# Routing tables of a fused attention and mixture-of-experts kernel: joined on VectorE instead of GpSimd, with earlier first weights for expert 0

## The chip, the cores and the metric

One core of one Trainium2 chip runs the whole kernel. The metric is device time of that core in microseconds, the median of several executions.

## What is computed

Eight batches of eight heads of attention over 576 positions with 64 elements each. Four heads see the last 32 positions, four see every fourth of the last 128. The result is read as 4608 rows of 512 elements, and each row goes through one of eight experts, the one with the largest gate logit:

```python
logits = x @ w_gate
expert_idx = np.argmax(logits, axis=1)
...
    xe = x[mask]
    h = np.maximum(xe @ w1[e], 0.0)
    ye = h @ w2[e]
    out[mask] = gate_w[mask, None] * ye
```

`w1[e]` is 512x1024, `w2[e]` is 1024x512, `gate_w` the softmax probability of the chosen expert.

## The kernel before

**Attention.** Two batches form a pair, four pairs (`NPR`) of nine tiles (`NT`) of 128 positions: 36 steps (`total`). `step(n)` (L1102) is a hand-written software pipeline: scores of tile n, softmax and transposes of n-1, products with v of n-2, transposes of the finished rows x of n-3, gate logits of n-4. TensorE, VectorE and ScalarE keep the written order in the first 35 steps (`MEND`, L1154); GpSimd and SP, and all engines from step 35 on, get their order from the framework's scheduler, which goes by readiness and by place in the program. Within a step, small jobs are pulled from lists: `side` (routing, pulled by `pull_off` and `pull_pe`), `slow` (scatters, two a step), `spare` (weight splits, one a step).

**Routing.** `route(m)` (L455) runs once per pair, from step 12, 21, 30 and 39. It turns the logits, finds the expert, counts the places within each expert with three matrix products, and for pairs 0 to 2 scatters (row number, gate) into three tables in device memory, `tabs`, in turn (L524, with the place computed by `place`, L518). Three tables are there so that a scatter waits only for the third one before it; empty entries are zero, so that the tables are joined by adding. The last pair takes another way: for each of its nine tiles `mark` (L536) makes two one-hot operands, `s1` (L539, from `ca`) and `b1` (L547), `enter` (L552) multiplies them on TensorE into the PSUM tile `tb`, VectorE scales `tb` (L634, L638) and adds it to the joined rows, which gives `row_i` (L639; the trace shows that line as L428). From `row_i` all experts but the first blocks of expert 0 gather their rows (L735).

**The tables.** `read_table` (L648) reads the three tables on SP's queue into `t_in[0..2]`, 128x320x2 int32 (row and gate). `add_tables` (L653) joins them with three GpSimd instructions: t0+t1 (L656), rows (L657), gates into `base` (L658). `read_all` (L1049) calls both behind the last scatter of pair 2. The gates of the last pair are scattered on their own later (L641); `all_gates` (L660) reads these into `scr`, `none` and `gall` and adds them to `base` on GpSimd. `early_fetch` (L1053) does the same join for 2 columns after pair 1, for expert 0's first two blocks; the change leaves that.

**Expert weights.** Weights are split into a high and a low part, so that three products of reduced precision make one of full precision. `Static.load` (L805) brings 128x1024 (512 KB) on SP's queue into one of three `raw` buffers. During attention expert 0's units 0 to 3 are loaded (`early_load`, L1074) at steps 24, 26, 28, 30 and split two steps later (`early_split`, L1077): `split_later` (L715) puts two halves per unit on `spare`, each with a ScalarE cast (L721) and a GpSimd subtraction (L724). Units 4 to 6 are loaded at steps 36 to 38. Four groups of expert 0's first layer run at steps 37 to 40 (`early_layer1`), before `row_i` is known. All later splits are a ScalarE cast (L709) and a VectorE subtraction (L710). The rows gathered are turned on TensorE (L785, L885) and split by ScalarE (L788) and VectorE (L792).

Of the kernel before, what the change touches and what calls it, by code (L numbers as in the profile page):

```python
# [11 lines left out]
I32 = mybir.dt.int32  # L12
BF16 = mybir.dt.bfloat16
AF = mybir.ActivationFunctionType
ALU = mybir.AluOpType
# [28 lines left out]
NBK = NE * BPE  # L44
# [106 lines left out]
def attention_moe_kernel(ctx, tc, qk, v, wg, w, cst, tok, end, slots, mask, zero, out):  # L151
# [14 lines left out]
    base = const.tile([P, NBK], F32, name="base")  # L166
# [4 lines left out]
    scr = const.tile([P, NBK], F32, name="scr")  # L171
    none = const.tile([P, NBK], F32, name="none")
    row_i = const.tile([P, NBK], I32, name="row_i")
# [14 lines left out]
    t_in = [late.tile([P, NBK, 2], I32, name=f"t_in{i}") for i in range(3)]  # L188
# [9 lines left out]
    total = NPR * NT  # L198
# [225 lines left out]
    def on_pe(f, *a, late=False):  # L424
        side.append((2 if late else 1, lambda: f(*a)))

    def off_pe(f, *a, **k):
        side.append((0, lambda: f(*a, **k)))  # L428

    def off_both(*fs):  # L430
        side.append((0, lambda: [f() for f in fs]))

    def spaced(f, *a):
        slow.append(lambda: f(*a))
# [20 lines left out]
    def route(m, then=None, after=None):  # L455


        v = nc.vector
# [72 lines left out]
        def scatter_gate(t):  # L531
            scatter(t, gtabs, gate[:, t : t + 1])
# [73 lines left out]
        if m < NPR - 1:  # L606
            off_both(
                lambda: v.tensor_tensor(load[:, :, 0], rows_i[:, m], plc_i, op=ALU.subtract),
                lambda: v.tensor_copy(load[:, ::3, 0], rows_i[:, m, ::3]),
                lambda: v.tensor_scalar_mul(wide, posf, float(NBK)),  # L610
            )

            def enter_pair():
                v.tensor_tensor(crun, crun, cs[:, :, NT - 1], op=ALU.add)
                for t in range(NT):
                    spaced(scatter, t, tabs, load[:, t])
                if then:
                    spaced(then)

            off_pe(enter_pair)  # L620
        else:
            off_both(
                lambda: v.tensor_copy(blk, blk_i),
                lambda: v.tensor_copy(plc, plc_i),
                lambda: v.tensor_tensor(pay, rows_f, plc, op=ALU.subtract),
            )
            off_pe(lambda: v.tensor_tensor(crun, crun, cs[:, :, NT - 1], op=ALU.add))
            for lo in range(0, NT + 3, 3):
                for t in range(lo, min(lo + 3, NT)):
                    off_pe(mark, t)  # L630
                if lo:
                    on_pe(enter, range(lo - 3, lo), late=True)
            off_pe(
                lambda: v.tensor_scalar(  # L634
                    scr, box["tb"], 0.0, float(LAST), op0=ALU.is_gt, op1=ALU.mult
                )
            )
            off_pe(lambda: v.tensor_tensor(scr, box["tb"], scr, op=ALU.add))  # L638
            off_pe(v.tensor_tensor, row_i, t_in[0][:, :, 0], scr, op=ALU.add)  # L639
            off_pe(lambda: v.tensor_scalar_mul(wide, posf, float(NBK)))  # L640
            for t in range(NT):  # L641
                gates_later.append(lambda t=t: scatter_gate(t))
# [5 lines left out]
    def read_table(n):  # L648

        for tab, to in zip(tabs, t_in):  # L650
            nc.sync.dma_start(to[:, :n], tab[:].rearrange("(p b) o -> p b o", p=P)[:, :n])

    def add_tables(rows, gates, n):  # L653

        t0, t1, t2 = [t[:, :n] for t in t_in]
        nc.gpsimd.tensor_tensor(t0, t0, t1, op=ALU.add)  # L656
        nc.gpsimd.tensor_tensor(rows, t0[:, :, 0], t2[:, :, 0], op=ALU.add)  # L657
        nc.gpsimd.tensor_tensor(gates.bitcast(I32), t0[:, :, 1], t2[:, :, 1], op=ALU.add)  # L658
# [385 lines left out]
    def at(n, f, *a):  # L1044
        todo.setdefault(n, []).append(lambda: f(*a))
# [2 lines left out]

    def read_all():  # L1049
        read_table(NBK)  # L1050
        add_tables(t_in[0][:, :, 0], base, NBK)

    def early_fetch():  # L1053
        def fetch():
# [9 lines left out]
    for m in range(NPR):  # L1064
        last = (m + 1) * NT - 1 + 4
        if m == EARLY - 1:
            at(last, route, m, early_fetch, reserve)
        elif m == NPR - 2:
            at(last, route, m, read_all)
        else:  # L1070
            at(last, route, m)
# [6 lines left out]
        first.units.append(split_later(u // 4, early.pop(u), 2))  # L1078

    for u in range(4):  # L1080
        at(total - 12 + 2 * u, early_load, u)
        at(total - 10 + 2 * u, early_split, u)
    for u in range(4, 7):
        at(total + u - 4, early_load, u)

# [151 lines left out]
    for i in range(NE):  # L1237
# [99 lines left out]
        if i == 1:  # L1337
# [9 lines left out]
                op=ALU.is_gt,  # L1347
# [10 lines left out]
                op=ALU.is_gt,  # L1358
# [127 lines left out]
```

## Time and profile before

| what | value |
|---|---|
| median of 3 runs (lowest, highest) | 648.47 us (648.32, 651.66) |
| the profiled execution's own time | 647.01 us |
| its span, first to last instruction | 645.2 us |
| TensorE busy | 611.1 us (95%) |
| VectorE busy | 360.5 us (56%) |
| ScalarE busy | 315.7 us (49%) |
| GpSimd busy | 244.1 us (38%) |
| mean granted TensorE clock | 0.987 of full speed |

In the profile PE is TensorE's products and PEld its weight loads, DVE is VectorE, ACT ScalarE, POOL GpSimd, SP the queue of SyncE; a q behind a name means its sequencer. L634 is line 634 of the kernel. A timeline row has the start, the time it spans, engine, line, operation, output and inputs, how many instructions are merged in the row, and in brackets the idle time before it with what ended it. Merged rows span all their instructions. The ends of matrix products are modelled.

### The profile page before, as it was taken

To read this page: it belongs to the slowest core of one execution; us is meant where nothing else is said; L and a number is where in the kernel's file an instruction comes from. 1 tells how busy PE (TensorE), PEld (TensorE's weight loads), DVE (VectorE), ACT (ScalarE), POOL (GpSimd) and SP (SyncE) were. 2 spreads that over 40 slices of the span, in tenths; PEclk is the share of its full clock that TensorE was granted. 3 is DMA by queue.
4 is the path that set the end of the run, shared out by engine and by line. 5 is a ranking of instruction groups with operands and counts; after the bars stand their busy time and mean duration, and the time that the engine had idled before them with its cause. 6 is when DMAs were issued, how large, how long until landed. Compare 5 with 4: busy or idle time off the path is not lost. (4 is left out here: it accounts for less than half of the span.)

```text
span 645.2 us, 13227 instructions
## 1 busy us (share of the span) xinstructions
PE 611.1 (95%) x5227; PEld 488.7 (76%) x5227; DVE 360.5 (56%) x783; ACT 315.7 (49%) x606; POOL 244.1 (38%) x292
## 2 busy tenths in 40 slices
PE   7999999998989989969999999999999999999993
PEld 5767777776768868848887888887888888888772
DVE  4867987889593466954664446356436544542100
ACT  3666667677534365133664456355436544642110
POOL 0333375598755510161054105312610541143511
PEclk9999999999999999969999999999999999999998
DMA  9999999985326563163566277536645762736620
GB/s 338 411 400 413 399 407 385 299 258 176 115 65 234 187 223 128 49 203 123 196 216 208 71 259 241 163 117 230 218 137 201 229 237 71 228 124 239 227 88 22
DMA packets 42847, 137.70 MB, mean 213 GB/s; under 512 B 8624, under 2 KB 10160, under 8 KB 42736
## 3 DMA queue, kind: packets, MB, share of 16 engines
q1 hardware_dynamic: 23232, 78.33, 34.4%
q0 software_dynamic: 19552, 58.51, 26.6%
q8 instruction: 42, 0.69, 0.4%
q14 instruction: 21, 0.17, 0.1%
HBM read 117.51 MB, written 21.30 MB: 215 GB/s over the span
## 5 line engine op out<-in xcount | busy, mean ns | idle before, releaser
L710 DVE TENSOR_TENSOR wu<-raw,wu 128x512 fp32r<-128x512 f32 x200 | 129.3, 692 | 91.8 <-ACT wu L709 86.7
L829 PE MATMUL hps<-x,wu 128*128 128x512 f32 (+1 forms) x720 | 166.5, 388 | 5.3 <-DVE h L841 4.6
L860 PE MATMUL yps<-wu,h 128*128 128x512 f32 x696 | 166.3, 394 | 0.0
L829 PEld LDWEIGHTS hps<-x,wu 128*128 128x128 f32 x720 | 132.9, 190 | 34.8 <-DVE h L841 6.2
L860 PEld LDWEIGHTS yps<-wu,h 128*128 128x128 f32 x696 | 129.5, 188 | 29.4 <-issue 0.8
L709 ACT CAST wu<-raw 128x512 fp32r<-128x512 f32 x200 | 113.0, 618 | 69.3 <-DMA raw<-in_w_dram,wi 36.1
L746 POOL DMA_INDIRECT out_dram<-y,row_i x30 | 31.0, 1035 | 155.8 <-ACT y L745 121.8
L841 DVE SCALAR_TENSOR_TENSOR h<-hps,h 128x512 fp32r<-128x512 f32 (+1 forms) x60 | 39.7, 671 | 75.5 <-ACT h L840 75.5
L840 ACT ACTIVATE h<-hps 128x512 fp32r<-128x512 f32 (+1 forms) x60 | 34.4, 582 | 81.2 <-PE hps L829 71.8
L314 ACT COPY pts<-pt 96x512 f32<-96x512 f32 x72 | 42.0, 583 | 49.0 <-PE pt L309 48.7
L894 POOL DMA_INDIRECT raw<-in_w_dram,wi x40 | 41.4, 1034 | 46.2 <-DVE wu L710 33.1
L735 POOL DMA_INDIRECT xg<-x_d,row_i x30 | 30.5, 1017 | 60.4 <-PE tpx L885 47.3
L745 ACT ACTIVATE y<-yps,gall 128x512 f32<-128x512 f32 x28 | 19.2, 687 | 68.8 <-PE yps L860 40.4
L288 DVE TENSOR_REDUCE nm<-s 128x4 f32<-128x384 f32 x72 | 39.5, 550 | 23.0 <-PE s L277 21.9
L309 PE MATMUL pt<-ident,p 128*96 128x128 f32 x288 | 46.1, 283 | 1.8 <-ACT pts L314 1.8
L356 POOL DMA_DIRECT2D x_d<-xs x36 | 20.5, 571 | 70.4 <-DVE xs L344 49.5
L945 PE MATMUL ypd<-wu,hd 128*128 128x512 f32 x168 | 44.1, 404 | 0.0
L293 DVE TENSOR_TENSOR d<-s,nm 128x384 f32<-128x384 f32 x72 | 40.0, 557 | 4.6
L324 PE MATMUL o<-vr,pts 96*64 96x65 f32 x1152 | 41.5, 224 | 0.0
L324 PEld LDWEIGHTS o<-vr,pts 96*64 96x64 f32 x1152 | 36.6, 137 | 6.6 <-issue 5.5
L303 ACT ACTIVATE p<-d 128x384 f32<-128x384 f32 x72 | 37.6, 524 | 7.4 <-DVE d L293 7.3
L913 PE MATMUL hpd<-wu,xd 128*128 128x512 f32 x168 | 40.5, 394 | 0.0
(170 smaller groups left out, 699.1 us busy)
## 6 DMA issues: line engine op xcount, KB each, us to landing
raw<-in_w_dram SPq DMA_DIRECT2D x64, 512.0 KB
qkr<-in_qk_dram SPq DMA_DIRECT2D x36, 576.0 KB
vr<-in_v_dram SPq DMA_DIRECT2D x36, 520.0 KB
x_d<-xs POOLq DMA_DIRECT2D x44, 128.0 KB
t_in<-tab SPq DMA_DIRECT2D x3, 320.0 KB
x_d<-xs POOLq DMA_DIRECT2D x8, 112.0 KB
x_d<-xs POOLq DMA_DIRECT2D x8, 96.0 KB
tab<-in_zero_dram SPq DMA_DIRECT2D x2, 320.0 KB
```

Source lines behind the costliest of these rows:

```text
L293: nc.vector.tensor_tensor(st["d", n][:, g], st["s", n][g], st["nm", n][:, g].broadcast_to([P, HP, KB]), op=ALU.subtract,)
L309: nc.tensor.transpose(pt[:KB, h], st["p", n][:, g, h], ident)
L314: nc.scalar.copy(st["pts", n][:, g], st.pop(("pt", n))[:KB])
L324: nc.tensor.matmul(st["o", n][QB * j : QB * (j + 1), g, h], lhsT=pts[:, g, h, QB * j : QB * (j + 1)], rhs=vr[:KB, n % NRV, a : a + DH + 1] ...
L709: nc.scalar.copy(u[:, 0, sl], raw[:, sl])
L710: nc.vector.tensor_tensor(u[:, 1, sl], raw[:, sl], u[:, 0, sl].bitcast(F32), op=ALU.subtract)
L829: nc.tensor.matmul(hps[:, : self.ns], lhsT=u[:, wpart, fs], rhs=self.x[:, xpart, c, : self.ns], start=(k == 0), stop=(k == 11),)
L841: nc.vector.scalar_tensor_tensor(h[:, 1, :n], hps[:, :n], 0.0, h[:, 0, :n].bitcast(F32), op0=ALU.max, op1=ALU.subtract,)
L860: nc.tensor.matmul(yps, lhsT=self.h[f][:, hpart, ts], rhs=u[:, wpart, fs], start=f == 0 and k == 0, stop=f == 7 and k == 2,)
L894: nc.gpsimd.indirect_dma_start(out=raw, out_offset=None, in_=w, in_offset=bass.IndirectOffsetOnAxis(ap=self.wi[:, u : u + 1], axis=0),)
L913: nc.tensor.matmul(hps, lhsT=self.x[:, xpart, c], rhs=u[:, wpart, ns], start=(k == 0), stop=(k == 11),)
L945: nc.tensor.matmul(self.yps, lhsT=self.h[f // 4][:, hpart, f % 4], rhs=u[:, wpart, fs], start=f == 0 and k == 0, stop=f == 7 and k == 2,)
```

## The change

The join of the three tables leaves GpSimd. In `route`, for the last pair, VectorE gets four instructions: an OR of t1 and t2 (rows) into the memory of `none`, a sum of that with t0 (rows), both written behind the one-hot operands and ahead of the scaling of `tb`; and, behind `row_i`, two ORs that join the gates into `base`. Since an entry stands in one table only and the others are zero there, OR joins like addition. `read_all` only reads. Apart from that, the loads and splits of expert 0's units 0 to 3 come two steps sooner (loads at steps 22, 24, 26, 28, splits at 24, 26, 28, 30).

```diff
--- before.py
+++ after.py
@@ -630,13 +630,25 @@
                     off_pe(mark, t)
                 if lo:
                     on_pe(enter, range(lo - 3, lo), late=True)
+            t0, t1, t2 = t_in
+            sum_ = none.bitcast(I32)
+            off_pe(v.tensor_tensor, sum_, t1[:, :, 0], t2[:, :, 0], op=ALU.bitwise_or)
+            off_pe(v.tensor_tensor, sum_, t0[:, :, 0], sum_, op=ALU.add)
             off_pe(
                 lambda: v.tensor_scalar(
                     scr, box["tb"], 0.0, float(LAST), op0=ALU.is_gt, op1=ALU.mult
                 )
             )
             off_pe(lambda: v.tensor_tensor(scr, box["tb"], scr, op=ALU.add))
-            off_pe(v.tensor_tensor, row_i, t_in[0][:, :, 0], scr, op=ALU.add)
+            off_pe(v.tensor_tensor, row_i, sum_, scr, op=ALU.add)
+            off_pe(v.tensor_tensor, t0[:, :, 1], t0[:, :, 1], t1[:, :, 1], op=ALU.bitwise_or)
+            off_pe(
+                v.tensor_tensor,
+                base.bitcast(I32),
+                t0[:, :, 1],
+                t2[:, :, 1],
+                op=ALU.bitwise_or,
+            )
             off_pe(lambda: v.tensor_scalar_mul(wide, posf, float(NBK)))
             for t in range(NT):
                 gates_later.append(lambda t=t: scatter_gate(t))
@@ -1048,7 +1060,6 @@
 
     def read_all():
         read_table(NBK)
-        add_tables(t_in[0][:, :, 0], base, NBK)
 
     def early_fetch():
         def fetch():
@@ -1078,8 +1089,8 @@
         first.units.append(split_later(u // 4, early.pop(u), 2))
 
     for u in range(4):
-        at(total - 12 + 2 * u, early_load, u)
-        at(total - 10 + 2 * u, early_split, u)
+        at(total - 14 + 2 * u, early_load, u)
+        at(total - 12 + 2 * u, early_split, u)
     for u in range(4, 7):
         at(total + u - 4, early_load, u)
```

## Rows read from the trace of the kernel before

**Rows 1.** Busy time by stretch: length, engines, clock, DMA share, GB/s.
```profile
158.20:162.20 4.00, 1.50 (x26) 1.19 (x20) 4.00 (x10) 1.73 (x5) 3.33 (x4) 1.00 0.47 152
162.20:177.40 15.20, 14.94 (x167) 12.60 (x167) 7.42 (x28) 8.17 (x19) 11.28 (x15) 1.00 0.37 101
177.40:187.00 9.60, 7.28 (x47) 5.96 (x45) 9.27 (x32) 0.87 (x3) 4.83 (x4) 1.00 0.12 35
187.00:200.00 13.00, 12.97 (x62) 10.43 (x63) 7.91 (x17) 5.93 (x13) 6.04 (x6) 1.00 0.70 233
200.00:226.70 26.70, 26.70 (x136) 22.12 (x135) 11.85 (x23) 11.68 (x22) 17.12 (x18) 1.00 0.55 177
```

**Rows 2.** TensorE's waits, 90 to 170 and 174 to 200 us: total, times, longest.
```profile
PE tpx L785 <- DVE x L792: 2.5, 1, 2.5
PE pt L309 <- ACT pts L314: 1.2, 3, 0.5
...
PE tb L558 <- DVE s L539: 1.5, 2, 1.1
PE tb L558 <- DVE b L547: 0.5, 1, 0.5
```

**Rows 3.** Single lines: xcount, ns minimum/median/maximum, first and last start.
```profile
L518 DVE SCALAR_TENSOR_TENSOR at_i<-blk_i,wide x7: 145/151/1894, 157.2 to 159.5; 128x1 int32<-128x1 int32 x7
...
L724 POOL TENSOR_TENSOR wu<-raw,wu x8: 1279/1284/1292, 127.3 to 158.2; 128x512 fp32r<-128x512 f32 x8
...
L602 DVE CAST pos<-posf x4: 174/175/1193, 76.9 to 178.2; 128x9 int32<-128x9 f32 x4
...
L539 DVE TENSOR_SCALAR s<-ca,plc,pay x9: 332/339/1052, 180.5 to 185.7; 128x128 fp32r<-128x128 f32 x9
```

**Rows 4.** GpSimd in order of time, 120 to 190 us.
```profile
120.02 0.57 POOL L356 DMA_DIRECT2D x_d<-xs  x1 [3.11 <-DVE at_i L518]
...
158.25 1.28 POOL L724 TENSOR_TENSOR wu<-raw,wu 128x512 fp32r<-128x512 f32 x1
...
173.31 1.03 POOL L524 DMA_INDIRECT tab<-load,at_i  x1 [0.30 <-issue]
...
177.71 1.61 POOL L656 TENSOR_TENSOR t_in<-t_in,t_in 128x640 int32<-128x640 int32 x1 [2.25 <-DMA t_in<-tab]
...
180.54 1.14 POOL L657 TENSOR_TENSOR t_in<-t_in,t_in 128x320 int32<-128x320 int32 x1 [1.23 <-DMA t_in<-tab]
181.64 1.02 POOL L658 TENSOR_TENSOR base<-t_in,t_in 128x320 int32<-128x320 int32 x1
...
189.65 1.52 POOL L735 DMA_INDIRECT xg<-x_d,row_i  x1 [5.72 <-DVE row_i L428]
```

**Rows 5.** VectorE in order of time, 159 to 191 us.
```profile
159.62 1.01 DVE L288 TENSOR_REDUCE nm<-s 128x4 f32<-128x384 f32 x2
...
178.15 1.19 DVE L602 CAST pos<-posf 128x9 int32<-128x9 f32 x1
179.26 0.16 DVE L640 TENSOR_SCALAR last_f<-posf 128x9 f32<-128x9 f32 x1
...
180.48 2.26 DVE L539 TENSOR_SCALAR s<-ca,plc,pay 128x128 fp32r<-128x128 f32 x3
...
188.89 0.49 DVE L428 TENSOR_TENSOR row_i<-t_in,scr 128x320 int32<-128x320 int32 x1
...
189.62 1.28 DVE L710 TENSOR_TENSOR wu<-raw,wu 128x512 fp32r<-128x512 f32 x2
```

**Rows 6.** TensorE in order of time, the turn of the first gathered rows.
```profile
197.27 0.60 PE L885 MATMUL tpx<-ident,xg 128*128 128x128 f32 x4
```

**Rows 7.** SP's queue in order of time, the reads of the tables.
```profile
171.28 6.57 SPq L651 DMA_DIRECT2D t_in<-tab  x3
```

**Rows 8.** Weight loads on SP's queue, 0 to 100 and 95 to 176 us.
```profile
L808 SPq DMA_DIRECT2D raw<-in_w_dram x3: 466/582/653, 70.4 to 88.0; - x3
...
L808 SPq DMA_DIRECT2D raw<-in_w_dram x4: 327/330/333, 133.6 to 159.6; - x4
```

## The prediction

> **What bounds the kernel now.** I read the stretches first, since the shares of the whole run are means over stages: for each stretch I compared TensorE's busy time with its length. From 162.2 to 177.4 us and from 187 us on TensorE is full (14.94 of 15.20, 12.97 of 13.00, 26.70 of 26.70 us), so whatever arrives sooner there gains nothing by itself, while a shift of TensorE's start is kept [rows 1]. Two stretches have holes: 158.2 to 162.2 (1.50 of 4.00 us busy) and 177.4 to 187 (7.28 of 9.60) [rows 1]. Then I read who ended TensorE's waits. In the first hole it waits 2.5 us for the low half of expert 0's turned rows (L792); in the second 1.5 us for the one-hot operand `s1` (L539) and 0.5 us for `b1` (L547), all from VectorE [rows 2]. So at the change the path runs through VectorE, and the question is what VectorE does in these moments.
>
> The rows of VectorE and GpSimd, laid side by side, answer that. In the first hole one of seven single-element place computations (L518) takes 1.89 us where the median takes 0.15 [rows 3]; GpSimd runs its last weight subtraction (L724) from 158.25 for 1.28 us, thus to 159.53, and VectorE's next reduction starts at 159.62 [rows 4, 5]. In the second hole the cast of `pos` (L602) runs 1.19 us from 178.15, to 179.34, while GpSimd adds tables (L656) until 179.32 [rows 4, 5]; the same cast at its median takes 0.175 [rows 3]. Three `s1` (L539) take 2.26 us from 180.48, to 182.74, beside GpSimd's L657 and L658, which end at 182.66 [rows 4, 5]; the median of the nine is 0.339 and the longest 1.052 [rows 3]. VectorE stands still until GpSimd's instruction ends: that is what these rows have in common.
>
> **The change part by part.** Removed: three GpSimd additions (1.61, 1.14 and 1.02 us, L656 to L658) [rows 4]. Nothing on GpSimd waits behind them except one gate scatter; the row gathers that follow wait until 189.65 for `row_i` anyway [rows 4]. Worth is the lock on VectorE. The cast gets 1.19 - 0.175 = 1.0 us back. The three `s1` would take about 3 x 0.3 = 0.9 at the spacing of unlocked ones (an estimate from the median 0.339, of which some overlaps), so 1.3 us return. VectorE gains 2.3 us ahead of the last one-hot operand. TensorE can take only what it waited there: 1.5 + 0.5 = 2.0 us [rows 2]. I take 2.0 (**-2.0**; bounds 0, if another wait moves in, to -2.3).
>
> Added: four VectorE instructions on 128x320 int32 (the sum of rows was there before, as one). The nearest row is the present `row_i` addition of the same shape: 0.49 us [rows 5]. The operation is another (bitwise OR), and no row shows one; bounds are half of it (0.25) and double (1.0), and I take 0.49 for its same size and stride. The first two (OR of t1 and t2, sum with t0) are due ahead of the scaling of `tb`. They fit behind the last operand: VectorE ends its operands 2.3 us sooner, TensorE only 2.0 us, and TensorE still has the last matrix products of `tb` to do, so VectorE has some time free there; I cost these two at nothing. Without that cover they cost 2 x 0.49 = 1.0 us. The last two (gates) come behind `row_i`, at 189.4, in the middle of the splits of second-layer weights (L710, two in 1.28 us from 189.62) [rows 5], which TensorE eats as they come: 0 to 1.0 us, and I take the middle, **+0.5**. The gathers after `row_i` have their cover: the first goes at 189.65, takes 1.52 us, and its rows are turned at 197.27 [rows 4, 6].
>
> The added wait: L656 and L657 waited for `t_in` on GpSimd; now VectorE waits. The third table is the late one: its last scatter starts at 173.31, the three reads on SP's queue last from 171.28 to 177.85, and L657, which needs the third table, starts at 180.54 after a wait of 1.23 us [rows 4, 7]. If the OR stands behind the operands, as written, the table is there. If not, everything behind it on VectorE waits, operands included (the rivals below).
>
> Moved: four loads of 512 KB on SP, eight casts on ScalarE (L721) and eight subtractions on GpSimd (L724), each two steps earlier. On SP three of the four loads are issued from 70.4 to 88.0 us already, far ahead of their use, and the fourth at 133.6 as soon as a `raw` buffer comes free [rows 8]; two steps change nothing for TensorE, and the loads of units 4 to 6 (to 159.6) only come sooner [rows 8]. On ScalarE the casts cost at most what TensorE waited for ScalarE's copies over the whole stretch from 90 to 170: 1.2 us in three waits [rows 2]; the same number of casts stays in the attention steps, so I take 0 (bounds -0.5 to +0.5, the longest of the three). On GpSimd the eight run from 127.3 to 158.2 [rows 3]; two steps earlier (about 9 us, since the eight, one a step, start 31 us apart, seven times 4.4) the last one ends near 150. That frees VectorE at 158.25: 1.89 - 0.15 = 1.7 us, of which I take 1.5, as the place computation had some 0.2 us to do in any case (**-1.5**; bounds 0 to -2.5, the whole wait). The first two land near 118 and 123, where GpSimd idles 3.11 us before 120.02 [rows 4], so the scatters there are not pushed by more than that. TensorE does not wait for VectorE between 90 and 156 [rows 2]; therefore the new place is costed at 0, bound +1.5.
>
> Here a rule speaks against the moved part. The row shows one instruction of VectorE held for 1.74 us by a subtraction [rows 3], and TensorE's only waits for VectorE between 90 and 170 are the 2.5 us behind it [rows 2]. The Trainium skill (SBUF — State Buffer, "Who interferes with whom") says that the port pair of VectorE and GpSimd is an exclusive lock, held for a whole instruction, and that the order of issue decides who blocks. By it a moved subtraction still blocks somebody, only in another step: the sum would be -1.5 instead of -3.0. The trace agrees on the block itself (the cast ends within 0.02 us of L656).
>
> The sum: -2.0 - 1.5 + 0.5 = -3.0 us. The profiled execution took 647.01 us with a span of 645.2; the sum made against it gives 644.0. The median of the three runs, 648.47, stands 1.5 us above the profiled time, so I forecast **645.5** against the median. It is carried to the end because TensorE is full from 187 to 226.7 and what follows hangs on it. Half a per cent, 3.2 us, is about what can be told from no change; the forecast lies just inside.
>
> **The rivals.**
> Third table, sooner with the rest (648.4, no change). After the 35th step the order on VectorE is not the written one: L640 is written behind `row_i` and runs at 179.26, ahead of the first `s1` at 180.48 [rows 5]. If the OR is put there too, it starts with the table at 180.54 instead of 178.3. Two instructions end at 181.5; the chain goes on 2.2 us later than the 179.34 of before, gets 1.3 back from the `s1`, and ends 0.9 later; with +0.5 and -1.5 that is -0.1. Against it: the OR is written behind the operands, and nothing has to stand still for it.
> Third table, not sooner (**649.9**, slower). The same place, but the scatters of the third table wait for earlier scatters to land and not for GpSimd's time, so the table comes at 180.54 in absolute time while VectorE is there 1.5 us sooner. Then the -1.5 is eaten: +0.9 + 0.5 = +1.4. It decides from the point at which L651's third read starts later than VectorE reaches the OR.
> The lock only moves (647.0). The subtractions hold VectorE in steps 25 and 26 (counting from 0) as they did in 34, TensorE pays 1.5 there: -2.0 + 0.5 = -1.5. For it: the lock's length; against it: no wait of TensorE for VectorE in the eight steps that have them now, but for the last [rows 2].
> Last, the order after step 35 may change in a way that no row shows; I allow 3 us to either side.
>
> **How the numbers follow.** Forecast 0.45; third table with the rest 0.20; third table late 0.12; lock moves 0.13; new order 0.10. The forecast's own range is -4.8 (both gains at their far bounds, nothing for the ORs: 643.7) to -1.5 (the first two ORs uncovered, the last two in full: 647.0). About 0.25 of its 0.45 lies past half a per cent, and with half of the last case faster is 0.30; slower takes 0.05 of the last and 0.07 of the late table, 0.12; same is 0.58. The range reaches from 643.5, past which 0.08 is left, to 649.9, past which about 0.1 is left.
>
> **What would show it.** No GpSimd table instruction between 175 and 185; the cast of `pos` at 0.2 us; all nine `s1` near 0.34; TensorE's waits for `s1` and `b1` gone; no L518 over 1 us near 158 and TensorE's wait at L785 down from 2.5 to about 1.0; five 128x320 instructions on VectorE of about half a microsecond, the first two behind the ninth operand. I am wrong if VectorE idles for `t_in` ahead of the operands, if an L518 or a cast near 115 to 125 takes over a microsecond and TensorE waits behind it, or if second-layer products wait for L710 by more than 1 us.

## The result, and the profile after

The change makes the kernel slower: median 656.45 us against 648.47, ratio 1.0111 with a 95% interval of 1.0079 to 1.0143. The profiled execution took 656.45 us with a span of 654.7, 9.5 us above the span of before. How far this holds on other chips is shown below.

Line numbers of after are higher: L797 is L785 of before, L804 L792, L736 L724, L841 and L853 are L829 and L841, L663 is L651, L722 L710. All joins carry L428, as `row_i` does.

VectorE in order of time, after, the answer to [rows 5] (columns as there):

```profile
168.21 0.42 DVE L853 SCALAR_TENSOR_TENSOR x<-s,x 128x256 fp32r<-128x256 f32 x1 [1.06 <-ACT x L852]
177.67 0.49 DVE L428 TENSOR_TENSOR t_in<-t_in,t_in 128x320 int32<-128x320 int32 x1 [9.04 <-DMA t_in<-tab]
178.08 0.42 DVE L853 SCALAR_TENSOR_TENSOR x<-s,x 128x256 fp32r<-128x256 f32 x1
180.39 0.49 DVE L428 TENSOR_TENSOR none<-t_in,t_in 128x320 int32<-128x320 int32 x1 [1.89 <-DMA t_in<-tab]
180.80 0.48 DVE L428 TENSOR_TENSOR base<-t_in,t_in 128x320 int32<-128x320 int32 x1
181.20 0.48 DVE L428 CUSTOM_DVE_ANT_0 none<-t_in,none 128x640 uint16<-128x640 uint16 x1
181.60 0.25 DVE L477 TENSOR_REDUCE lt<-tl 128x24 f32<-128x96 f32 x1
...
186.97 0.17 DVE L602 CAST pos<-posf 128x9 int32<-128x9 f32 x1
...
188.31 0.85 DVE L539 TENSOR_SCALAR s<-ca,plc,pay 128x128 fp32r<-128x128 f32 x3
...
195.32 0.48 DVE L428 TENSOR_TENSOR row_i<-none,scr 128x320 int32<-128x320 int32 x1
```

The four joins stand not behind the one-hot operands but ahead of the last pair's whole routing, which begins with L477. The first to run is an OR of gates, which in the program is written behind `row_i`. It needs the first two tables and waits 9.04 us; the OR of rows needs the third and waits 1.89 more. Together 10.9 us in which VectorE stands, with everything queued behind it.

TensorE in order of time, after:

```profile
160.44 0.66 PE L797 MATMUL tpx<-ident,xg 128*128 128x128 f32 x4 [0.98 <-DVE x L804]
...
171.87 0.82 PE L472 MATMUL tl<-ident,lgs 128*128 128x128 f32 x6
178.55 0.58 PE L841 MATMUL s<-x,wu 128*128 128x256 f32 x1 [5.86 <-DVE x L853]
181.91 0.90 PE L472 MATMUL tl<-ident,lgs 128*128 128x128 f32 x3 [2.77 <-DVE lt L477]
...
194.99 3.23 PE L872 MATMUL yps<-wu,x 128*128 128x512 f32 x12
```

TensorE waits 5.86 us for a result of the early first layer (L853) that stands on VectorE behind the first join, then 2.77 us for `lt`, the turned logits, which stands behind all four. The stretches of after answer to [rows 1] (columns as there):

```profile
162.20:171.90 9.70, 9.70 (x117) 7.88 (x114) 3.05 (x8) 6.14 (x14) 7.43 (x10) 1.00 0.13 33
171.90:178.60 6.70, 0.84 (x9) 0.59 (x7) 0.83 (x2) 0.38 (x1) 4.30 (x7) 0.84 0.67 190
178.60:188.70 10.10, 7.33 (x39) 6.91 (x39) 6.63 (x32) 0.65 (x2) 0.80 (x1) 0.60 0.06 24
188.70:233.10 44.40, 44.02 (x225) 36.21 (x225) 24.26 (x56) 18.47 (x36) 23.31 (x24) 1.00 0.54 177
```

From 171.9 to 178.6 TensorE is busy 0.84 us of 6.70, and behind that hole the granted clock is 0.60, a mix of the levels 1.2 and 2.4 GHz. `row_i` comes at 195.32, where it was 188.89 [rows 5]: 6.4 us later. The rest of the 9.5 us (3.1) comes after `row_i`; about half of it shows as one stretch, 21.0 us long at a clock of 0.92 in after and 19.6 us at 1.00 before:

```profile
244.70:265.70 21.00, 21.00 (x86) 17.10 (x86) 13.80 (x22) 11.06 (x21) 0.00 (x0) 0.92 0.41 134
```

```profile
237.90:257.50 19.60, 19.57 (x86) 15.81 (x86) 13.73 (x22) 11.44 (x21) 0.00 (x0) 1.00 0.44 147
```

Both expected gains are there all the same. The last pair's cast L602 takes 0.17 us, no `s1` is slow (the first three 0.85 us together, 2.26 in [rows 5]), the waits for `s1` and `b1` are gone, and the wait for the second turned rows fell from 2.5 [rows 2] to 0.98 us.

### The profile page after: what moved, and what is told of

Same layout as the page of the kernel before. It is cut to its first block, busy times and chain, and to the rows that moved or that the text cites. A ratio compares the mean times of both kernels' runs of the same rounds, so it can differ in the third digit from the quotient of the medians.

```text
span 654.7 us, 13225 instructions
## 1 busy us (share of the span) xinstructions
PE 617.3 (94%) x5227; PEld 494.1 (75%) x5227; DVE 358.0 (55%) x787; ACT 315.1 (48%) x606; POOL 241.8 (37%) x289
## 5 line engine op out<-in xcount | busy, mean ns | idle before, releaser
L722 DVE TENSOR_TENSOR wu<-raw,wu 128x512 fp32r<-128x512 f32 x200 | 129.0, 690 | 97.4 <-ACT wu L721 95.3
L841 PE MATMUL hps<-x,wu 128*128 128x512 f32 (+1 forms) x720 | 169.1, 392 | 6.2 <-DVE h L853 5.5
L841 PEld LDWEIGHTS hps<-x,wu 128*128 128x128 f32 x720 | 134.5, 192 | 36.7 <-DVE h L853 7.8
L853 DVE SCALAR_TENSOR_TENSOR h<-hps,h 128x512 fp32r<-128x512 f32 (+1 forms) x60 | 39.6, 669 | 74.9 <-ACT h L852 74.9
```

Source lines behind the costliest of these rows:

```text
L722: nc.vector.tensor_tensor(u[:, 1, sl], raw[:, sl], u[:, 0, sl].bitcast(F32), op=ALU.subtract)
L841: nc.tensor.matmul(hps[:, : self.ns], lhsT=u[:, wpart, fs], rhs=self.x[:, xpart, c, : self.ns], start=(k == 0), stop=(k == 11),)
L853: nc.vector.scalar_tensor_tensor(h[:, 1, :n], hps[:, :n], 0.0, h[:, 0, :n].bitcast(F32), op0=ALU.max, op1=ALU.subtract,)
```

## The experiments

The theory: the price is VectorE's wait for the tables at the place where the scheduler puts the joins. The rivals: the early weights do harm, the joins are dear by themselves, or it was that one run. The kernels ran on four chips, A to D, each beside the kernel before on the same chip; a ratio is to that.

### Chip A (before: 651.32 us)

**Joins tied by data.** Each join takes the result of the one before as an operand, and the first takes the scaled `tb`, so that none can run ahead of it. There are as many instructions as in the change, but the rows now cost three additions behind each other, and all three stand behind the scaling of `tb`, where the change has one. The early weights stay.

```diff
-            off_pe(v.tensor_tensor, sum_, t1[:, :, 0], t2[:, :, 0], op=ALU.bitwise_or)
-            off_pe(v.tensor_tensor, sum_, t0[:, :, 0], sum_, op=ALU.add)
...
+            off_pe(v.tensor_tensor, sum_, t0[:, :, 0], scr, op=ALU.add)
+            off_pe(v.tensor_tensor, sum_, t1[:, :, 0], sum_, op=ALU.add)
+            off_pe(v.tensor_tensor, row_i, t2[:, :, 0], sum_, op=ALU.add)
+            part = scr.bitcast(I32)
+            off_pe(v.tensor_tensor, part, t0[:, :, 1], t1[:, :, 1], op=ALU.bitwise_or)
+            off_pe(v.tensor_tensor, base.bitcast(I32), part, t2[:, :, 1], op=ALU.bitwise_or)
```

> The joins stay on VectorE and the weights stay early, but each join is tied to the one-hot result by its data: rows are t0 + scaled tb, then + t1, then + t2, and the first OR of the gates is written over the scaled tb. So none can run before the last one-hot product. Wait theory (the change lost its time because VectorE stood at joins placed far ahead of the one-hot operands, for tables that had not landed): no VectorE wait for t_in, both gains that were forecast show (TensorE's second wait at the turn down to 1.0 us, no TensorE wait for the one-hot operands), at most 2 us of joins among the weight splits are paid, 645.5 to 648. Work theory (the join instructions themselves, or the earlier weights, cost the time): 653 or more.

Measured: 646.67 us, ratio 0.9918 (0.9887 to 0.995). VectorE in order of time, joins tied:

```profile
176.22 0.17 DVE L602 CAST pos<-posf 128x9 int32<-128x9 f32 x1
...
184.58 0.48 DVE L428 TENSOR_TENSOR none<-t_in,scr 128x320 int32<-128x320 int32 x1
185.31 0.48 DVE L428 CUSTOM_DVE_ANT_0 none<-t_in,none 128x640 uint16<-128x640 uint16 x1
185.71 0.48 DVE L428 TENSOR_TENSOR scr<-t_in,t_in 128x320 int32<-128x320 int32 x1
186.11 0.49 DVE L428 CUSTOM_DVE_ANT_0 row_i<-t_in,none 128x640 uint16<-128x640 uint16 x1
186.52 0.48 DVE L428 TENSOR_TENSOR base<-scr,t_in 128x320 int32<-128x320 int32 x1
```

and TensorE's waits from 158 to 200 us in the same kernel (total, times, longest):

```profile
PE yps L867 <- DVE wu L717: 1.6, 1, 1.6
PE tpx L792 <- DVE x L799: 0.5, 1, 0.5
```

No wait for a table is left, and the kernel with the same joins in another place is 0.8% faster than before. How much of that is due to the joins, the next runs show. Their price is the 1.6 us that TensorE waits for the splits behind them.

**The early weights alone** (the change without its joins).

> The kernel before with nothing but the earlier loads and splits of expert 0's units 0 to 3; GpSimd joins as before. Wait theory: a gain of 0.5 to 1.8 us (the VectorE instruction held at 158 us is gone), 646.7 to 648. If the earlier weights are what costs: 653 or more. If the lock only moves to steps 25 and 26: 648.5.

Measured: 647.7 us, ratio 0.9929 (0.9904 to 0.9953). The early weights do no harm; they carry most of the gain.

**The joins alone**, as the change has them, with the loads and splits at their old steps, and **the tied joins alone**.

```diff
-        at(total - 14 + 2 * u, early_load, u)
-        at(total - 12 + 2 * u, early_split, u)
+        at(total - 12 + 2 * u, early_load, u)
+        at(total - 10 + 2 * u, early_split, u)
```

> The changed kernel with the loads and splits of expert 0 put back to their old steps; joins on VectorE as in the change. Wait theory: VectorE still stands for t_in ahead of the routing of the last pair, 8 us or more in all, and the table lands a little later, 655 to 659. If the earlier weights are what costs: 648 to 650.

> The tied joins of the first experiment with the old steps of the weights. Wait theory: gain 2.0 us from the lock and up to 2 us paid for the joins among the weight splits, 646.5 to 649; the difference to the first experiment is what the earlier weights are worth beside tied joins, 0.5 to 1.8 us. Work theory: 653 or more.

Measured: 656.41 us and 1.0081 (1.0055 to 1.0107) for the joins as written, 650.68 us and 0.9992 (0.996 to 1.0024) tied. The two kernels have as many joins each and differ in their place, and their intervals lie apart: the place costs 5.7 us. VectorE in order of time, joins alone, as written:

```profile
171.78 0.42 DVE L853 SCALAR_TENSOR_TENSOR x<-s,x 128x256 fp32r<-128x256 f32 x1 [1.05 <-ACT x L852]
177.66 0.49 DVE L428 TENSOR_TENSOR t_in<-t_in,t_in 128x320 int32<-128x320 int32 x1 [5.46 <-DMA t_in<-tab]
178.07 0.42 DVE L853 SCALAR_TENSOR_TENSOR x<-s,x 128x256 fp32r<-128x256 f32 x1
180.78 0.49 DVE L428 TENSOR_TENSOR none<-t_in,t_in 128x320 int32<-128x320 int32 x1 [2.29 <-DMA t_in<-tab]
```

The first join starts at 177.66 here, at 177.67 in the changed kernel, and GpSimd's first join before the change at 177.71 [rows 4]. In these three kernels the first two tables come at the same moment, and VectorE, where it gets there sooner, only waits longer (9.04 us against 5.46). The join that needs the third table starts at 180.78, 180.39 and 180.54, so that one agrees within 0.4 us. With the early weights alone GpSimd's joins start at 178.69 and 180.99, each after a wait for its table; to the microsecond the moment holds there too, not closer.

Why the early weights are worth more than I gave them shows in the tied joins with old weights. TensorE in order of time:

```profile
162.93 0.66 PE L792 MATMUL tpx<-ident,xg 128*128 128x128 f32 x4 [2.51 <-DVE x L799]
163.43 0.94 PE L309 MATMUL pt<-ident,p 128*96 128x128 f32 x4
164.30 2.00 PE L324 MATMUL o<-vr,pts 96*64 96x65 f32 x32
...
168.79 1.16 PE L324 MATMUL o<-vr,pts 96*64 96x65 f32 x32
```

and two of its stretches:

```profile
162.80:165.50 2.70, 2.57 (x30) 2.20 (x32) 1.09 (x6) 1.54 (x4) 1.91 (x2) 0.64 0.15 44
165.50:167.50 2.00, 2.00 (x24) 1.75 (x20) 1.12 (x4) 0.26 (x1) 1.87 (x3) 0.64 0.04 5
```

Behind the hole of 2.5 us the clock falls to 0.64 for some four microseconds, and 32 products that take 1.16 us at 168.79 take 2.00. In the profile of before the same hole was followed by a clock of 1.00 [rows 1]; with the early weights the hole is short and the clock stayed up. Over all profiles, a hole of 2.1 to 2.5 us at this place was followed by such slow products in three (the 32 products take 2.00 here, 1.72 with the joins alone, 1.98 in the kernel before on chip B) and by a clock of 1.00 in two (before, first and on chip D). Behind the holes of 0.5 to 1.6 us of the tied joins, the changed kernel and the early weights alone it stayed at 1.00. What follows the long hole thus differs between executions; that the early weights gain by this is read from these profiles, and no run tests it by itself.

### Chip B (before: 658.33 us)

**Rows tied, gate ORs free; gates tied, rows free; joins written into buffers that come free late.** The first two use the halves of the diff above. The third writes the sums into the ring of `b1` buffers, so that they cannot start before the products that read these are done:

```diff
+            def ring():
+                return sp.tile([P, NBK], F32R, name="b1", bufs=6).bitcast(I32)
```

> Rows tied to the one-hot result as in e1, the two ORs of the gates left free as in the change; in program order on VectorE they stand ahead of the routing of the last pair, the three additions of the rows behind it. Wait theory: one free join is enough, since VectorE keeps its order and everything behind waits for the same landing: 8 us or more of VectorE idle for t_in, ratio to the kernel before 1.005 to 1.015. Count theory (each free join costs its own wait or work, so half the joins cost half): ratio 0.998 to 1.004.

> The reverse: gates tied behind the rows, the OR and the addition of the rows left free as in the change. The OR needs the third table at once. Wait theory: VectorE idles until the third table lands near 180.4 us, ratio 1.005 to 1.015, as with the gates. Count theory: 0.998 to 1.004.

> All joins as in the change (four instructions), but the OR of the rows and the first OR of the gates write into buffers of the one-hot operand b1, which come free only when early one-hot products are done. So they can't run ahead of the operands, and they run before the second-layer weight splits and not among them. Wait theory: no VectorE wait for t_in over 1 us, TensorE's 1.6 us wait for the split of e1 shrinks by 1 us or more, ratio 0.985 to 0.993, the best so far. If e1's additions were no burden: the same as e1, 0.992. If joins ahead of the scaling of tb hold up the fifth group of the first layer: slower than e1, 0.993 to 0.998.

> The kernel before once more with a profile, on the chip of these runs, so that stretches are compared on one chip. Nothing should differ from the first profile up to 285 us by more than 1 us; if the whole run is 2 to 3 us longer, as on the last chip, the profile should show where.

Measured: 1.0031 (0.9999 to 1.0064), 1.0027 (0.9997 to 1.0056) and 1.0012 (0.997 to 1.0054); the kernel before, profiled there, 658.39 us. Either half alone, left free, still waits: VectorE's waits from 150 to 200 us with gates free, then with rows free:

```profile
DVE t_in L428 <- DMA t_in<-tab: 6.6, 1, 6.6
...
DVE base L428 <- issue: 1.6, 1, 1.6
```

```profile
DVE none L428 <- DMA t_in<-tab: 7.0, 1, 7.0
```

So both halves run ahead, and TensorE waits 5.1 us for it (3.2 and 1.9) in the one and 6.0 us in the other. The ring removes VectorE's wait, but its joins then stand ahead of a first-layer result, for which TensorE waits 2.1 us. That none of these is told apart from before by its time was not expected, and led to the next runs.

### Chip C (before: 659.1 us)

**Idle products in the hole.** The changed kernel with 40 products of 128x256 that nobody reads, behind the third early group, to keep TensorE at work where it waited 5.9 us; and the changed kernel, the tied joins and the ring again.

```diff
+        if f == 2:
+            idle = psa.tile([P, 512], F32, tag="T", name="idle")
+            for _ in range(40):
+                nc.tensor.matmul(
...
```

> The changed kernel with 40 extra 128x256 products on TensorE (40 x 0.14 = 5.6 us, their result read by nobody) behind the third early group of the first layer, where TensorE stands idle for 5.9 us. VectorE's wait for the tables stays as it is. If part of the loss is the clock that falls in the hole (0.60 of full between 178.6 and 188.7 us in the changed kernel): granted clock 1.0 there, and 1 to 3 us faster than the changed kernel of the same chip. If the clock costs nothing because VectorE's chain sets the end: the same as the changed kernel, within 0.5 us.

> The changed kernel once more, so that it, its filled form and both tied forms are compared on one chip. Slower than the kernel before by 0.5 to 1.4%, with VectorE idle for t_in for over 8 us in all.

> The tied joins of e1 once more beside the changed kernel on the same chip. Wait theory: 1.2 to 2.2% faster than the changed kernel (its 10.9 us of waits less the 1.6 us that the joins cost among the weight splits), 0.3 to 1.0% faster than the kernel before.

> The joins in the buffers of the one-hot operand once more, beside e11 on the same chip, since e7 had a chip on which the stretch from 164 to 180 us is 4 us longer in the kernel before too. If the 1.6 us that TensorE waits for the weight split in e1 are what these joins save: 1 to 1.6 us faster than e11. If the joins ahead of the first-layer group give it back: the same within 0.7 us.

Measured: 0.9974 (0.9945 to 1.0002), 0.9976 (0.9945 to 1.0008), 0.9999 (0.9977 to 1.002), 1.0014 (0.9985 to 1.0043). Here the change costs nothing that the time shows, and the tied joins, which I expected 1.2 to 2.2% below it, win nothing either. VectorE in order of time, changed kernel, chip C:

```profile
177.66 0.42 DVE L853 SCALAR_TENSOR_TENSOR x<-s,x 128x256 fp32r<-128x256 f32 x1
180.01 0.50 DVE L428 TENSOR_TENSOR t_in<-t_in,t_in 128x320 int32<-128x320 int32 x1 [1.94 <-DMA t_in<-tab]
180.42 0.43 DVE L853 SCALAR_TENSOR_TENSOR x<-s,x 128x256 fp32r<-128x256 f32 x1
182.22 0.49 DVE L428 TENSOR_TENSOR none<-t_in,t_in 128x320 int32<-128x320 int32 x1 [1.38 <-DMA t_in<-tab]
```

The joins stand in the same place, directly behind the same L853. But that L853 ran at 168.21 in the first trace and runs at 177.66 here, 9.4 us later, while the tables come only 1.8 to 2.3 us later. What is left of the wait is 3.3 us, and TensorE waits 0.6 for it. The idle products had no hole to fill; that run says nothing of the clock. It shows something else. TensorE in order of time, with the idle products:

```profile
182.51 4.96 PE L1104 MATMUL idle<-x,wu 128*128 128x256 f32 x40
187.31 0.82 PE L472 MATMUL tl<-ident,lgs 128*128 128x128 f32 x6
```

They hold up the last turns of logits by 4.96 us. The second layer starts at 199.87, in the changed kernel on this chip at 195.47, and yet the medians are 657.81 and 658.42 us: from that start to the end the one profile takes 455.4 us and the other 462.2. Here 4.4 us at this place do not show in the time, so equal times do not prove that a wait is gone.

### Chip D (before: 658.61 us)

**The changed kernel, the tied joins, the kernel before and the idle products, side by side.**

> The changed kernel once more, on whatever chip this is. Theory (the joins run ahead of the operands, and VectorE waits there for the third table, unless the table has landed before it gets there): where the kernel before takes about 650 us, VectorE waits over 8 us for t_in and the ratio is 1.008 to 1.014; where it takes about 658 us, the waits sum to under 4 us and the ratio is within 0.4% of 1. Rival (the loss of the first run was a chance of that run): the ratio is within 0.4% of 1 or below at either.

> The four joins tied by data behind the operands, early weights kept, beside the changed kernel on the same chip. Theory: where the kernel before takes about 650 us, 0.990 to 0.995 and at least 1.2% below the changed kernel; where it takes about 658 us, within 0.4% of the changed kernel. Rival: the two are within 0.4% at either.

> The kernel before, profiled on the same chip. If the stand-still of all engines between 165 and 178 us goes with chips on which the kernel before takes about 658 us, its profile shows it there (the last of the products tl after 180 us, and a wait of some 3 us on VectorE, ScalarE and GpSimd together) and on a chip with about 650 us it doesn't (tl ends at 174 to 177 us).

> The changed kernel with 40 products of 128x256 that nobody reads behind the last early group of the first layer. If the hole of the first trace is there (TensorE waits 5.9 us for x at L841) the products fill it, the granted clock behind it is 0.95 or more where it was 0.60, and the time is 2 to 4 us below the changed kernel's on the same chip. Rival (the loss is VectorE's wait alone, the clock gives it no more): within 1 us of it. Where no such hole is, they come on top and the run tells nothing.

Measured: the changed kernel 659.0 us, 0.9999 (0.997 to 1.0028); tied 657.62 us, 0.9968 (0.9939 to 0.9997); before, profiled, 659.25 us; idle products 0.9995 (0.9967 to 1.0023), again without the hole they were for, and so silent. In the changed kernel VectorE waits 2.96 and 2.34 us for tables, more than the 4 us I expected in sum, and TensorE 1.5 us for `lt`. The tied joins are 0.3% faster than the kernel before, as far as that can be told. The idle products stand behind the third early group, as on chip C, and not behind the last, as I wrote. VectorE in order of time, kernel before, chip D:

```profile
173.12 0.17 DVE L334 TENSOR_SCALAR z<-o 128x8 f32<-128x8 f32 x1 [3.76 <-remote]
...
178.18 0.17 DVE L334 TENSOR_SCALAR z<-o 128x8 f32<-128x8 f32 x1 [3.47 <-PE s L829]
```

and TensorE and ScalarE in the same kernel:

```profile
169.41 1.15 PE L324 MATMUL o<-vr,pts 96*64 96x65 f32 x32
...
174.81 1.15 PE L324 MATMUL o<-vr,pts 96*64 96x65 f32 x32 [0.50 <-issue]
...
184.60 0.55 PE L472 MATMUL tl<-ident,lgs 128*128 128x128 f32 x3
```

```profile
173.18 0.58 ACT L314 COPY pts<-pt 96x512 f32<-96x512 f32 x1 [2.62 <-remote]
```

The products `o` end at 170.56 and 175.96 by the profile, and VectorE, which reads them, starts 2.6 and 2.2 us later, ScalarE beside it within 0.06 us. All twelve profiles of chips B, C and D show such a late start for the first of these two products, by 1.7 to 5.0 us; the six of the first measurement and chip A have 0.05. But only part of the difference lies here. The last turn of logits starts at 184.60, 10.1 us later than in the first profile of before (174.46), and 6.6 of these were there when the first gathered rows of expert 0 were turned (163.08 against 156.51); on chip B it is 5.2 of 8.8 us. That VectorE comes late to the joins hides the wait for the tables. That it is the only thing that hides it is not shown, since the idle products on chip C disappeared too, and here the tied joins start the second layer 6.2 us before the changed kernel (190.83 against 197.00) for medians 1.4 us apart.

## Why the prediction was wrong

**The failed step** is "They fit behind the last operand", costed "at nothing", with "If the OR stands behind the operands, as written, the table is there". The joins do not stand where they are written. From step 35 on the scheduler orders VectorE by readiness, as the front part says, and I used that in the rivals alone. What I needed to ask was what each join waits for: three tables that any instruction behind the reads may ask for. Nothing of the last pair's routing is an operand of the four. Tying them to `tb` moved them back and took the loss away (0.9918 on chip A, with the joins alone 0.9992 instead of 1.0081), which shows the place as the cause there.

**The rivals on the third table** had the right mechanism at the wrong place and price. I moved only the two row joins, and only ahead of the operands at 178.3, for 2.2 us. In the trace all four stand ten microseconds further up, gates first. VectorE is one queue in order (the Trainium skill says so in "DVE: scalar operands, raw-bit mode, write accounting and state across instructions", section 5, "Flops that outlive an instruction"; the trace agrees: L477 runs at 181.60, 0.4 us behind the last join, though `tl` had been on TensorE since 171.87). So the wait blocked the early first layer and the routing as well. That the table comes "in absolute time", the core of the rival that I gave 0.12, holds over three kernels within 0.05 us for the first two tables and 0.4 for the third.

**The size.** Against the tied kernel of chip A the second layer starts 10.7 us later in the first trace (194.99 against 184.25). TensorE's two waits are 5.86 + 2.77 = 8.6. The way from the last turn of logits to the first product of `tb` takes 6.80 us (181.91 to 188.71) instead of 5.44 (172.52 to 177.96) at the clock of 0.60, 1.4 more. The start of the second turn differs by 0.2. That leaves 0.5 unexplained. The two forms of the joins alone, both on chip A, give the same picture: 6.8 us (195.21 against 188.41), of which 5.1 are the two waits (2.28 and 2.82) and 1.2 the slower way (6.69 against 5.45). The clock's part is read from these profiles alone, since the runs meant to test it met no hole.

**The gains were right in kind.** In the tied kernel the second turn starts at 160.25, before at 162.21: 2.0 us (forecast 1.5). From there to the last products of `tb` another 2.4 us come in (181.53 against 185.85 is 4.3 in all; forecast 2.0). The 1.6 us for splits behind the joins stands where I wrote 0.5, with 1.0 as the bound; the tied form has four joins ahead of these splits besides the addition of before, where I counted two. The sum at the first 512-wide group of expert 0 (223.99 against 226.66) is -2.7 us where I had -3.0. On chip A the whole gain is 4.65 us, and the early weights alone gain 3.6 there (647.7 against 651.32), where I gave them 1.5. The half clock behind the long hole, which they avoid, may be the rest: tied joins with old weights reached the last turn of logits at 176.68, 2.2 us later than the profile of before (174.46), 0.7 of it there already at the second turn. The kernel before wasn't profiled on that chip, so that it suffers the same there is argued, not shown. The joins off GpSimd, for which I had a net 1.5 us, give 0.6 by themselves when tied (650.68 against 651.32, ratio 0.9992, 0.996 to 1.0024), which is told apart neither from nothing nor from 1.5.

**"The lock only moves"** (0.13) did not happen as I costed it: TensorE has no wait for VectorE from 90 to 170 but the 0.98 us. The rule I cited for it, the exclusive lock of the Trainium skill (SBUF — State Buffer, "Who interferes with whom"), still fits: one place computation L518 of the changed kernel, at 128.81, takes 1.16 us where the median is 0.15 and ends 0.03 us behind a subtraction, and TensorE does not wait for it. A part of the lock did move. I had the last subtraction end near 150; it starts at 155.63 and runs until 156.92, and a cast beside it, from 156.15, takes 0.81 us instead of 0.17. Single lines of the changed kernel (columns as in [rows 3]):

```profile
L736 POOL TENSOR_TENSOR wu<-raw,wu x8: 1285/1287/1301, 117.5 to 155.6; 128x512 fp32r<-128x512 f32 x8
L602 DVE CAST pos<-posf x4: 172/174/815, 77.4 to 187.0; 128x9 int32<-128x9 f32 x4
```

From there VectorE has no idle time until the result that TensorE waits 0.98 us for. With the tied joins on chip A this cast takes 0.35 us and the wait is 0.52, with the early weights alone 1.02 and 1.61.

**What stays open.** Two of the four chips ran the changed kernel itself, and neither lost time with it; chip A showed the loss with the joins alone. The first measurement and chip A have the kernel before at 648 to 651 us, the others at 658 to 659, and there VectorE comes late to the joins. Where most of that lateness comes from, ahead of 160 us, was not followed. Why VectorE gets TensorE's products up to 5.0 us late on those chips, ScalarE with it, is not settled; the profile names "issue" and "remote", and no run was made that could tell it.

## What to carry to other kernels

Where a scheduler goes by readiness, an instruction belongs where its operands put it, not where it is written: before moving work to an in-order engine, list what each instruction depends on, and if that is only a late transfer, tie it by data to the point where it is wanted. On chip A that took the joins alone from a loss of 0.8% to no measurable difference; the gain of 0.8% of the whole kernel there came mostly from the early weights (0.7% alone). A change that trades one wait for another should be measured on several chips, since a wait that cost 0.8% on one did not show in the time on others.

## What the runs showed of the hardware

A hole of 2.1 to 2.5 us on TensorE was followed by a clock of 1.00 in two executions and by three to four microseconds of slower products in three (a clock of 0.64 in one); a hole of 6.7 us with 0.84 us of work by ten microseconds at 0.60. An addition of two int32 tables shows as a custom VectorE instruction on 128x640 uint16 and takes 0.48 us, as long as the OR (0.49): the price taken for the OR was right. Between chips the same program had medians of 651.3 and 658 to 659 us; part of the difference lies between 165 and 178 us, where on chips B to D VectorE starts 1.7 to 5.0 us after the end that the profile models for TensorE's products, and 0.05 us after it on the others (on chip D, in the kernel before, VectorE at 173.12 and ScalarE at 173.18 us after an end at 170.56).
